# A chunked recurrence without levels, and experts' rows in groups of three tiles turned by VectorE

## The chip, the cores and the metric

The kernel runs on one core of one Trainium2 chip. The time is that of one execution on the device, in microseconds (us). Everything is float32.

## What is computed

Two blocks follow each other. The first is a gated linear recurrence over 4 batches x 8 heads, 768 tokens and a head dimension of 48; the second sends each of the 3,072 tokens (a row of 384 values, all heads side by side) to the one of eight experts with the largest logit.

```
f = 1 / (1 + exp(-f_logit))
for t in range(S):                       # per batch and head, state is 48 x 48
    state = f[t][:, None] * state + outer(k[t], v[t])
    y[t] = q[t] @ state
x = y as (3072, 384)
e = argmax(x @ w_gate)                   # w_gate: 384 x 8
out = softmax(x @ w_gate)[e] * (relu(x @ w1[e]) @ w2[e])   # w1: 384 x 1024, w2: 1024 x 384
```

## The kernel before, in words

**Recurrence (L146 to L373).** A chunk is 128 tokens of one batch, 24 in all, two batches half a chunk apart (`steps`, `advance`, L344 to L373). Tokens lie on partitions when loaded; `turned` (L178) transposes f, q and k on TensorE, two heads to a 128-row tile. Seven levels (L224) then build the scores: at each, four products of 128 columns (L227), the query factors multiplied on VectorE (L234), the key factors on GpSimd (L236), the block totals (L238), and a masked copy into the score tile (L240). Each level needs the factors of the one before. The chunk's outputs are eight products of the scores (L250) and, after the first chunk, eight of the state (L260); the state takes a transpose of the keys (L272), a product (L278) and a sum (L293). The rows are transposed again for the gate's logits (L301, L306).

**Routing (`route`, L309).** Once for each batch of six chunks: expert, place within the expert's region of a scratch tensor `xs` in memory, gate. Rows are scattered to `xs` by an indirect DMA that GpSimd issues (L130).

**Plan (L376 to L416).** After the last chunk a tile of padding is scattered behind each expert's rows, and VectorE works out for each of 31 tiles which expert and which row it has. 31 is the most that any routing can need; all run.

**Experts (L418 to L462).** Tile by tile: SyncE (SP) reads two registers and loads the tile's 128 rows and its expert's first weights (1.5 MB, L430); TensorE transposes the rows (L434); 24 products of 128 columns (L443), ReLU on ScalarE and VectorE, eight of 384 columns with second weights that were loaded during the recurrence (L457), the gate on VectorE (L461), a scatter to the output. The program's order on each engine is the order in which a scheduler took the statements as written.

Of the kernel before, what the change touches and what calls it, by code (L numbers as in the profile page):

```python
# [19 lines left out]
C = 128  # tokens in a chunk, and in a tile of an expert's rows  # L20
NC = S // C
HP = H // 2
DP = 64  # rows that a head takes in the layouts with the head dim on partitions
DM = H * D
KD = DM // 128
N = B * S
E, F = 8, 1024
NF = F // 128
LEVELS = [1 << i for i in range(7)]
STAGES = len(LEVELS) + 3  # of a chunk  # L30

REGION = N + C  # rows of an expert in the scratch: all tokens and a tile of padding
DUMMY = E * REGION  # a tile of padding rows for the tiles that no expert needs
ROWS = DUMMY + C
# [3 lines left out]
FAR = 1 << 20  # the token of a padding row  # L38


def _consts():
# [3 lines left out]
    def row(v):  # L45
# [8 lines left out]
        "eidx": row(e),  # L54
        "tiles": row(np.arange(N // C) * C),
        "i": row(np.arange(NT)),
        "irow": row(np.arange(NT) * C - DUMMY),
        "p": p[:, None],
    }
    # By level: columns are the second halves of the blocks of 2m tokens, rows  # L60
    # that count are the first half of the same block.
    m = {}
    for lv in LEVELS:
        t = p[p // lv % 2 == 1]
        m[lv] = (p[:, None] // (2 * lv) == t[None] // (2 * lv)) & (p[:, None] // lv % 2 == 0)
    m[0] = np.eye(128)
# [17 lines left out]
def kernel(  # L84
    ctx: ExitStack,
    tc: tile.TileContext,
    q: bass.AP,
    k: bass.AP,
    v: bass.AP,
    f_logit: bass.AP,  # L90
# [11 lines left out]
    nc.scalar.dma_start(fpack, nc.inline_tensor(fv, name="c_fpack").ap())  # L102
    nc.scalar.dma_start(mpack, nc.inline_tensor(mv, name="c_mpack").ap())
# [5 lines left out]
    def mask(lv):  # L109
        a, w = mat[lv]  # L110
        return mpack[:, a : a + w]

    ident = const("ident")

    xs = nc.dram_tensor("xs", (ROWS, ROW), F32, kind="Internal").ap()

    w2r = cpool.tile([128, E, NF, DM], F32, name="w2r")
    wg = cpool.tile([128, KD, E], F32, name="wg")
    nc.scalar.dma_start(wg, moe_w_gate.rearrange("(k p) e -> p k e", p=128))
    pad = cpool.tile([128, ROW], F32, name="pad")  # L120
    tok = cpool.tile([128, N // C], I32, name="tok")
    base = cpool.tile([128, B * NC + 1, E], F32, name="base")
# [366 lines left out]
```

## Time and profile before

| | us |
|---|---|
| median of three runs | 1058.12 |
| the three runs | 1054.77, 1085.23, 1058.12 |
| span of the profiled execution, first to last instruction | 1046.0 |
| recurrence and routing in it | 0 to 656 |
| last routing, padding, plan, first loads | 656 to 688 |
| 31 experts' tiles | 688 to 1038 |

The span leaves out what lies around the program's instructions; the profiled execution has no time of its own beside its span, so the runs stand for it. PE is TensorE's products and PEld its weight loads, which overlap them; DVE is VectorE, ACT ScalarE, POOL GpSimd and SP SyncE. A float32 product shows as two records of each kind.

### The profile page before, as it was taken

What the parts mean: (1) busy time and instruction counts of PE and PEld (TensorE: products, weight loads), DVE (VectorE), ACT (ScalarE), POOL (GpSimd) and SP (SyncE); (2) the same over time, 40 slices, a digit from 0 to 9 for tenths busy, and PEclk for the clock granted to TensorE, in tenths of its full rate; (3) what the DMA queues carried; (4) which work ended last, traced back from release to release, by engine and by line L of the source; (5) the groups of instructions that cost most, each with busy time, mean ns of one, the idle gap of its engine ahead of it and who ended that gap; (6) DMA issues with size and microseconds to landing.
All of it is one profiled execution on the core that took longest, in us unless ns stands there. A gap on an engine that the chain in (4) does not pass through costs nothing.

```text
span 1046.0 us, 13595 instructions
## 1 busy us (share of the span) xinstructions
PE 822.6 (79%) x5077; PEld 712.2 (68%) x5077; DVE 519.0 (50%) x1022; ACT 115.9 (11%) x205; POOL 207.4 (20%) x267
## 2 busy tenths in 40 slices
PE   5767777777776677777777777079999999999996
PEld 4667666667676666766776766067787787787775
DVE  7686777775666777667777763311111111111111
ACT  2020111111111211111111110000000000000000
POOL 2221222221214422222222213500010010010010
PEclk8797899996878799888899975579999999999999
DMA  9364112210112211111110001355445445545540
GB/s 224 129 213 150 31 31 42 41 33 17 22 31 78 71 31 39 29 25 31 31 31 8 1 0 48 110 213 205 161 154 188 181 158 191 174 155 175 190 157 1
DMA packets 129952, 99.27 MB, mean 95 GB/s; under 512 B 102734, under 2 KB 115313, under 8 KB 129888
## 3 DMA queue, kind: packets, MB, share of 16 engines
q1 hardware_dynamic: 125024, 86.58, 27.7%
q0 software_dynamic: 4032, 11.28, 3.0%
q8 instruction: 42, 0.69, 0.3%
q10 hardware_dynamic: 832, 0.54, 0.2%
q14 instruction: 22, 0.18, 0.1%
HBM read 86.90 MB, written 12.85 MB: 95 GB/s over the span
## 4 chain that ended last, share of the span: by engine, by line
issue 35%; DVE 30%; PE 28%; POOL 4%; DMA 1%; ACT 1%; SPq 0%; POOLq 0%; ACTq 0%
DVE qg L234 14%; PE lps L227 12%; DVE at L240 7%; PE y L250 5%; PE y L260 4%; DVE qg L221 3%; POOL out_dram L130 3%; DVE at L210 3%; DVE tots L238 2%; PE dp L278 2%; PE lp L306 2%; PE dps L207 1%; PE hps L443 1%; DMA w1t<-in_moe_w_dram 1%; POOL xs L130 1%
## 5 line engine op out<-in xcount | busy, mean ns | idle before, releaser
L227 PE MATMUL lps<-qg,kg 128*128 128x128 f32 x1344 | 240.7, 335 | 125.8 <-DVE qg L221 76.6
L227 PEld LDWEIGHTS lps<-qg,kg 128*128 128x128 f32 x1344 | 214.4, 239 | 147.6 <-issue 80.2
L234 DVE TENSOR_TENSOR qg<-qg,tots 64x256 f32<-64x256 f32 x288 | 161.1, 559 | 53.8 <-PE lps L227 50.0
L443 PEld LDWEIGHTS hps<-xT,w1t 128*128 128x128 f32 x1488 | 172.1, 194 | 20.9 <-DVE xT L436 11.4
L443 PE MATMUL hps<-xT,w1t 128*128 128x128 f32 x1488 | 175.2, 278 | 13.0 <-DVE xT L436 7.8
L236 POOL TENSOR_TENSOR kg<-kg,tots 128x256 f32<-128x256 f32 x140 | 110.1, 786 | 336.6 <-PE lps L227 296.6
L457 PE MATMUL yps<-w2r,hT 128*128 x496 | 165.1, 486 | 0.0
L240 DVE COPY_PREDICATED at<-mpack,lps 128x512 f32<-128x512 uint8 x168 | 148.0, 881 | 4.5
L457 PEld LDWEIGHTS yps<-w2r,hT 128*128 128x128 f32 x496 | 91.9, 190 | 57.5
L453 DVE TENSOR_SCALAR hT<-hps 128x512 f32<-128x512 f32 x31 | 21.4, 692 | 164.8 <-PE hps L443 90.1
L130 POOL DMA_INDIRECT out_dram<-ysb,xrow x31 | 30.1, 972 | 333.1 <-DVE ysb L461 307.5
L461 DVE TENSOR_SCALAR ysb<-yps,xrow 128x384 f32<-128x384 f32 x31 | 19.1, 617 | 136.2 <-PE yps L457 136.2
L250 PE MATMUL y<-vld,at 128*128 128x48 f32 x384 | 51.0, 289 | 24.6 <-DVE at L240 24.3
L250 PEld LDWEIGHTS y<-vld,at 128*128 128x128 f32 x384 | 47.9, 203 | 30.2 <-DVE at L240 30.2
L207 PE MATMUL dps<-qg,kg 128*128 128x256 f32 x192 | 50.8, 410 | 17.9 <-ACT kg L200 17.9
L451 ACT ACTIVATE hT<-hps 128x512 f32<-128x512 f32 x31 | 18.5, 597 | 356.6 <-PE hps L443 356.6
L207 PEld LDWEIGHTS dps<-qg,kg 128*128 128x128 f32 x192 | 36.7, 201 | 27.9 <-ACT kg L200 23.3
L234 DVE TENSOR_TENSOR qg<-qg,ft 64x256 f32<-64x256 f32 x48 | 32.3, 672 | 41.3 <-PE lps L227 40.5
L260 PE MATMUL y<-state,qg 128*128 128x48 f32 x320 | 48.1, 313 | 0.0
L260 PEld LDWEIGHTS y<-state,qg 128*128 128x128 f32 x320 | 46.2, 230 | 0.0
L236 POOL TENSOR_TENSOR kg<-kg,ft 128x256 f32<-128x256 f32 x24 | 23.9, 996 | 98.4 <-PE lps L227 98.4
L274 ACT COPY kn<-kp 128x512 f32<-128x512 f32 x20 | 11.7, 586 | 244.4 <-PE kp L272 244.4
(86 smaller groups left out, 567.0 us busy)
## 6 DMA issues: line engine op xcount, KB each, us to landing
w1t<-in_moe_w_dram SPq DMA_DIRECT2D x31, 1536.0 KB, 6.6
w2r<-in_moe_w_dram SPq DMA_DIRECT2D x8, 1536.0 KB, 8.7
xrow<-xs SPq DMA_DIRECT2D x31, 200.0 KB, 2.4
fld<-in_f_logit_dram SPq DMA_DIRECT2D x24, 192.0 KB, 2.7
qld<-in_q_dram SPq DMA_DIRECT2D x24, 192.0 KB, 3.2
kld<-in_k_dram SPq DMA_DIRECT2D x24, 192.0 KB, 2.8
vld<-in_v_dram SPq DMA_DIRECT2D x24, 192.0 KB, 2.7
out_dram<-ysb,xrow POOLq DMA_INDIRECT x31, 2.6
```

The lines of the kernel that those rows point to most:

```text
L130: ins = nc.gpsimd.indirect_dma_start(out=dst, out_offset=bass.IndirectOffsetOnAxis(ap=idx, axis=0), in_=src, in_offset=None, bounds_check= ...
L207: nc.tensor.matmul(ps[:, j], lhsT=kg[:, hp, :], rhs=qg[:, hp], start=True, stop=True)
L210: nc.vector.copy_predicated(at[:, 4 * g : 4 * g + 4, :], _bc(mask(0), 1, 4), ps.rearrange("p j a t -> p (j a) t"),)
L221: nc.vector.tensor_tensor(qg[r, :, a, :], qg[r, :, a, :], ft[r], op=OP.mult)
L227: nc.tensor.matmul(ps[:, hp], lhsT=kg[:, hp, :], rhs=half(qg[:, hp], m, 1), start=True, stop=True)
L234: nc.vector.tensor_tensor(q1, q1, _bc(two[r, :, :, 0], 3, m), op=OP.mult)
L236: nc.gpsimd.tensor_tensor(k0, k0, _bc(two[:, :, :, 1], 3, m), op=OP.mult)
L240: nc.vector.copy_predicated(half(at, m, 1), _bc(mask(m).rearrange("p (n r) -> p n r", r=m), 1, H), ps.rearrange("p h a (n r) -> p (h a) n ...
L250: nc.tensor.matmul(y[:, h * D : h * D + D], lhsT=at[:, h, :], rhs=vt[:, h * D : h * D + D], start=h == 0, stop=c == 0, skip_group_check=True,)
L260: nc.tensor.matmul(y[:, h * D : h * D + D], lhsT=qg[:, h // 2, h % 2, :], rhs=state[:, h // 2, :], start=False, stop=True, skip_group_chec ...
L443: nc.tensor.matmul(hp[:, f, :], lhsT=w1t[:, j, o : o + 128], rhs=xT[:, j, :], start=j == 0, stop=j == KD - 1,)
L457: nc.tensor.matmul(yp, lhsT=hT[:, f, :], rhs=w2r[:, ds(er, 1), f, :], start=f == 0, stop=f == NF - 1)
```

## The change

It is a new program for both stages; the fallback at its end is the only part that works as a loop on the chip.

- **Inputs** are laid out on the host: q, k and f come with the head dimension on partitions (a pair of heads, 64 rows each, zeros above 48), by units of 128 tokens x two batches x eight heads; v with tokens on partitions. There are 12 units; the transposes of q, k and f go.
- **Recurrence.** The levels go. Per unit: `steps` (ScalarE: exp, then ln, which gives -log f), `total` (VectorE: a running sum over each chunk's tokens), `growth` and `decay` (ScalarE: exp of the sum and of its negative), k times the one on GpSimd, q times the other on VectorE. One product for each head then gives its scores (`score`), copied through one causal mask. `keys` transposes k (TensorE), `keep` copies it (ScalarE), `within` and `before` write the outputs with the head dimension on partitions, `added` and `update` make the next state, `settle` copies the outputs (ScalarE), `rows` turns them back into rows together with their logits by one product with a matrix of ones and gate weights, `lay` copies the rows (ScalarE). Routing is by groups of two units (one at the end). The order on every engine is that of the statements: iteration n works on units n + 3 to n - 2.
- **Early tiles.** The first 128 rows of experts 0 and 1 are complete before the recurrence ends; their two tiles run in the last iterations and after them. Padding is written by SP, whose registers take each expert's end (`load_pads`).
- **Experts.** The expert of a tile is fixed: three tiles each, two for experts 0 and 1, one product of 384 (256) columns for the first weights, which are loaded once per expert, as the second ones are. Rows come from memory in blocks of 32 x 96 (`load_blocks`: four loads, and one for tokens and gates), which one VectorE transpose in squares of 32 turns (`turn`).
- **Spill.** An expert's rows beyond 384 go in squares of 32 rows. Two *quads* of four squares, each with its own expert's weights (3 MB a square), run beside experts 4 and 7: four products write 32 rows of the result each, eight transposes, four products again (`widen_quad`, `turn_quad`, `narrow_quad`; `fetch` loads them half an expert at a time).
- **Fallback.** A branch at the end reads a flag on all engines. The flag is set where a running sum or a routing goes beyond what the fixed program holds; then loops do it again.

The diff, cut to what sets the order and the sizes:

```diff
-LEVELS = [1 << i for i in range(7)]
...
-NT = N // C + E - 1  # the most tiles that any routing needs
...
+T = 32
+QUADS = 2
+SLOTS = 4 * QUADS
+SPILL = 4
...
+WITH = {4: 0, E - 1: 1}
+FETCH = {2: 0, 9: 1}
...
+EARLY = 2
...
+    def load_blocks(to, rows):
+        for j in range(128 // BK):
+            nc.sync.dma_start(
+                to[BK * j : BK * j + BK],
+                rows[:, DB * j : DB * j + DB].rearrange("(i c) m -> c i m", c=BK),
+            )
+    def load_rows(row, n=1):
+        rows = xs[ds(row, n * C)] if not isinstance(row, int) else xs[row : row + n * C]
+        x = rowp.tile([128, TILES * C // BK, DB], F32, name="xrow")[:, 0 : n * C // BK]
+        tg = rowp.tile([128, TILES, USED - TOK], F32, name="tg")[:, 0:n]
+        load_blocks(x, rows)
+        nc.sync.dma_start(tg, rows[:, TOK:USED].rearrange("(t p) r -> p t r", p=C))
+        return {"n": n, "x": x, "tg": tg}
...
+        nc.vector.transpose(
+            x["xT"].rearrange("p k (i c) -> p i k c", c=BK),
+            x["x"].rearrange("p i (r k) -> p i k r", k=KD),
+        )
...
+        per = 4 // n
+        for b in blocks:
+            i, f = divmod(b, per)
+            if f == 0:
+                x["h"] = bank(i)[:, 0 : per * n * C].rearrange("p (f c) -> p f c", f=per)
+            for j in range(KD):
+                nc.tensor.matmul(
+                    x["h"][:, f],
+                    lhsT=w[0][:, j, b * 128 : b * 128 + 128],
+                    rhs=x["xT"][:, j],
+                    start=j == 0,
+                    stop=j == KD - 1,
+                )
...
+    def put(x, t, yp, group):
+        ysb = ep.tile([128, DM], F32, name="ysb")
+        nc.vector.tensor_scalar(ysb, yp, x["tg"][:, t, 1:2], None, op0=OP.mult)
+        scatter(out, x["dst"][:, t : t + 1], ysb, N - 1, group)
...
+            g = x["g"][:, part, 1:CR]
+            most = gsum[:, u, 1 if part == ab[1] else 0]
+            nc.scalar.activation(
+                g, x["f"][:, part], AF.Exp, scale=-1.0, accum_out=most.unsqueeze(1)
+            )
+            nc.scalar.activation(g, g, AF.Ln, bias=1.0)
...
+            nc.vector.tensor_tensor_scan(
+                x["sum"][:, part].rearrange("p s c -> p (s c)"),
+                x["g"][:, part].rearrange("p s c -> p (s c)"),
+                cap[:, part].rearrange("p s c -> p (s c)"),
+                0.0,
+                OP.add,
+                OP.min,
+            )
...
+            nc.scalar.activation(x["r"][:, part], x["sum"][:, part, 1:CR], AF.Exp)
...
+        def by_r(u, part=whole):
+            k = units[u]["k"][:, part]
+            nc.gpsimd.tensor_tensor(k, k, units[u]["r"][:, part], op=OP.mult)
...
+            nc.scalar.activation(
+                x["dec"][:, part], x["sum"][:, part, 1:CR], AF.Exp, scale=-1.0
+            )
...
+            nc.vector.tensor_tensor(q, q, x["dec"][:, part], op=OP.mult)
...
+        def score(u, a):
+            x = units[u]
+            x["at"] = scores[u % 2]
+            ps = [pss.tile([128, HP, C], F32, name="s") for h in range(2)]
+            for p, h, r in heads():
+                s = HP * a + p
+                nc.tensor.matmul(
+                    ps[h][:, p], lhsT=x["k"][r, s], rhs=x["q"][r, s], start=True, stop=True
                 )
+            for h in range(2):
+                nc.vector.copy_predicated(x["at"][:, a, h], _bc(causal, 1, HP), ps[h])
...
+        def within(u, a):
+            x = units[u]
+            if a == 0:
+                x["yt"] = yt
+            for p, h, _ in heads():
                 nc.tensor.matmul(
+                    x["yt"][DP * (h ^ a) : DP * (h ^ a) + D, a, p],
+                    lhsT=x["v"][:, a, 2 * p + h],
+                    rhs=x["at"][:, a, h, p],
+                    start=p == 0,
+                    stop=x["old"] is None,
                     skip_group_check=True,
                 )
+        def before(u):
+            x = units[u]
+            if x["old"] is None:
+                return
+            for p in range(HP):
+                for h in range(2):
+                    for a in range(2):
+                        r = slice(DP * h, DP * h + D)
+                        to = DP * (h ^ a)
+                        nc.tensor.matmul(
+                            x["yt"][to : to + D, a, p],
+                            lhsT=x["old"][r, HP * a + p],
+                            rhs=x["q"][r, HP * a + p],
+                            start=False,
+                            stop=True,
+                            skip_group_check=True,
+                        )
+        def added(u):
+            x = units[u]
+            x["dp"] = turns("dp", [128, SEG, D])
+            for a in range(2):
+                for p, h, r in heads():
+                    s = HP * a + p
                     nc.tensor.matmul(
+                        x["dp"][r, s],
+                        lhsT=x["kn"][:, s, r],
+                        rhs=x["v"][:, a, 2 * p + h],
+                        start=s == 0,
                         stop=True,
                         skip_group_check=True,
                     )
...
+        for n in range(NU + 2):
+            here, back, last = n, n - 1, n - 2
+            rt = None
+            if here < NU:
+                units[here]["old"] = states[here % 2]
+            if 0 <= last:
+                settle(last)
+            if here < NU:
+                score(here, 0)
+            if 0 < n and n + 1 < NU:
+                by_r(n + 1)
+                ends(n + 1)
+            if later:
+                settled(*later)
+                later = None
+            if decayed:
+                decayed()
+                decayed = None
+            if sends:
+                now = sends if n >= NU - 1 else sends[:1]
+                for send in now:
+                    send()
...
+            elif here < NU:
+                if n == 1:
+                    added(0)
+                    decayed = update(0)
+                keys(here)
+                keep(here)
+                score(here, 1)
+            if 0 < n and n + 2 < NU:
+                total(n + 2)
+            if 0 <= last:
+                rt = rows(last)
+                if rt:
+                    rt.choose()
+            if 0 < n and n + 1 < NU:
+                decay(n + 1)
+                last_decay(n + 1)
+            if 0 < n and n + 3 < NU:
+                steps(n + 3)
+            if 0 <= last:
+                lay(last)
+            if rt:
+                rt.weigh()
+            if 0 < n and n + 2 < NU:
+                growth(n + 2)
+            for a in range(2):
+                if 0 <= back < NU:
+                    within(back, a)
+            if n == NU + 1:
+                widen(soon[0], weights[0], early_h, range(3, 7))
+            if n == NU:
+                for x in soon:
+                    turn_early(x)
+            if 0 <= back < NU:
+                before(back)
+            if 0 < n and n + 1 < NU:
+                for part in ab:
+                    by_decay(n + 1, part)
...
+            if 0 < here < NU and here // 2 < NC - 1:
+                added(here)
+                decayed = update(here)
+            if rt:
+                rt.count(turns("rp", [128, 2, rt.n, E], n < NU - 2))
+                later = (n, rt)
+                if n >= NU:
+                    settled(*later)
+                    later = None
+            if n == NU:
+                early_h = early_banks()
+                widen(soon[0], weights[0], early_h, range(3))
+            if n == NU + 1:
+                widen(soon[0], weights[0], early_h, range(7, NF))
+            if 0 < n and n + 3 < NU:
+                load(n + 3, "k")
+            if n + 2 < NU:
...
+            if n in (8, 10):
+                load_first_weights((n - 8) // 2)
+                load_second_weights((n - 8) // 2)
+            if n == NU - 1:
+                soon = [load_rows(first[e]) for e in range(EARLY)]
...
+        over, okc = share(), sums()
+        rows_of = {}
+        for e in range(E):
+            load_pads(e)
+            if e < 2:
+                rows_of[e] = load_expert(e)
+        narrow_early(soon[0], weights[0])
+        widen(soon[1], weights[1], early_banks(), range(NF))
+        check(okc, over)
+        turn(rows_of[0])
+        narrow_early(soon[1], weights[1])
...
+            hp = [bank(b).rearrange("p (f c) -> p f c", c=C) for b in range(2)]
+            hq = qp.tile([128, 2, 4, C], F32, name="hq")
+            for b in range(2):
+                for j in range(KD):
+                    for g, r in pieces():
+                        nc.tensor.matmul(
+                            hp[b][r].rearrange("p f c -> p (f c)"),
+                            lhsT=x["xT"][:, j, r],
+                            rhs=x["w"][0][:, g, j, b * 512 : b * 512 + 512],
+                            start=j == 0,
+                            stop=j == KD - 1,
+                            skip_group_check=True,
+                        )
...
+        for e in range(E):
+            x, w = rows_of[e], weights[e]
+            x["hT"] = qp.tile([128, NF, TILES * C], F32, name="hT")[:, :, 0 : x["n"] * C]
+            widen(x, w, bank, range(NF))
+            if e in WITH:
+                widen_quad(quad)
+            if e + 1 < E:
+                turn(rows_of[e + 1])
+            if e + 1 in WITH:
+                turn(quad, qp)
+            if e + 2 < E:
+                rows_of[e + 2] = load_expert(e + 2)
+                load_first_weights(e + 2)
+            fetch(2 * e)
+            for t in range(x["n"]):
+                if e in WITH and t == 1:
+                    turn_quad(quad)
+                if e in WITH and t == 2:
+                    narrow_quad(quad)
+                narrow_late(x, t, w)
+            if e + 2 < E:
+                load_second_weights(e + 2)
+            fetch(2 * e + 1)
+    todo = nc.values_load(fixi[0:1, 0:1], min_val=0, max_val=1)
+    with tc.If(todo > 0):
```

## Rows read from the trace of the kernel before

**Rows 1.** The page: busy us (share of span) by engine; granted clock, 40 slices.

```profile
PE 822.6 (79%) x5077; PEld 712.2 (68%) x5077; DVE 519.0 (50%) x1022; ACT 115.9 (11%) x205; POOL 207.4 (20%) x267
...
PEclk8797899996878799888899975579999999999999
```

**Rows 2.** Windows: us; PE, PEld, DVE, ACT, POOL busy; clock; DMA share; GB/s.

```profile
150.00:550.00 400.00, 296.35 (x1915) 272.67 (x1913) 283.29 (x561) 62.23 (x111) 103.12 (x131) 0.86 0.17 37
656.00:688.00 32.00, 2.19 (x8) 1.72 (x9) 7.32 (x33) 0.00 (x0) 13.72 (x14) 0.50 0.49 179
...
718.00:1030.00 312.00, 304.73 (x1854) 241.36 (x1853) 49.64 (x84) 16.13 (x27) 27.22 (x28) 1.00 0.48 168
```

**Rows 3.** The page: the chain that ended last, by engine and line.

```profile
issue 35%; DVE 30%; PE 28%; POOL 4%; DMA 1%; ACT 1%; SPq 0%; POOLq 0%; ACTq 0%
DVE qg L234 14%; PE lps L227 12%; DVE at L240 7%; PE y L250 5%; PE y L260 4%; DVE qg L221 3%; POOL out_dram L130 3%; DVE at L210 3%; DVE tots L238 2%; PE dp L278 2%; PE lp L306 2%; PE dps L207 1%; PE hps L443 1%; DMA w1t<-in_moe_w_dram 1%; POOL xs L130 1%
```

**Rows 4.** Waits: who waited for whom, us in total, times, longest.

```profile
PE lps L227 <- DVE qg L221: 76.6, 24, 3.3
```

**Rows 5.** Timeline, experts' tiles: start, us, engine, line, count.

```profile
687.74 7.96 PE L443 MATMUL hps<-xT,w1t 128*128 128x128 f32 x48 [5.18 <-issue]
...
802.59 5.52 PE L443 MATMUL hps<-xT,w1t 128*128 128x128 f32 x48
...
807.95 5.33 PE L457 MATMUL yps<-w2r,hT 128*128 x16
...
813.11 0.82 PE L434 MATMUL etp<-fpack,xrow 128*128 128x128 f32 x6
```

**Rows 6.** Timeline, products of 48 columns at either clock.

```profile
245.73 1.99 PE L250 MATMUL y<-vld,at 128*128 128x48 f32 x16 [1.54 <-DVE at L240]
...
620.87 3.61 PE L260 MATMUL y<-state,qg 128*128 128x48 f32 x16
```

**Rows 7.** Groups by form: busy us, mean ns | idle before, releasers.

```profile
L236 POOL TENSOR_TENSOR kg<-kg,tots 128x256 f32<-128x256 f32 x140 | 110.1, 786 | 336.6 <-PE lps L227 296.6 <-issue 26.3 <-DVE tots L238 6.8
...
L210 DVE COPY_PREDICATED at<-mpack,dps 128x512 f32<-128x512 uint8 x48 | 33.8, 724 | 4.9 <-PE dps L207 4.5
L221 DVE TENSOR_TENSOR qg<-qg,ft 64x512 f32<-64x512 f32 x48 | 32.6, 679 | 0.7
...
L130 POOL DMA_INDIRECT xs<-xr,posi x24 | 23.9, 994 | 13.7 <-DVE tots L238 5.5 <-issue 5.5 <-DVE posi L331 1.7
...
L274 ACT COPY kn<-kp 128x512 f32<-128x512 f32 x20 | 11.7, 586 | 244.4 <-PE kp L272 244.4
...
L268 ACT COPY xr<-y 128x384 f32<-128x384 f32 x24 | 11.5, 479 | 152.4 <-PE y L260 141.6 <-PE y L250 7.8 <-DVE at L240 3.0
...
L238 DVE TENSOR_TENSOR tots<-ft 128x256 f32<-128x256 f32 x24 | 10.0, 415 | 2.0 <-ACT ft L194 2.0
L287 POOL TENSOR_TENSOR state<-state,tots 128x192 f32<-128x192 f32 x16 | 8.6, 538 | 35.5 <-DVE tots L238 35.5
...
L314 DVE TENSOR_REDUCE mx<-lg 128x6 f32<-128x48 f32 x4 | 0.8, 204 | 0.1
```

**Rows 8.** Timeline, the end.

```profile
1037.61 0.49 PE L457 MATMUL yps<-w2r,hT 128*128 x1
...
1039.03 0.97 POOL L130 DMA_INDIRECT out_dram<-ysb,xrow  x1 [9.55 <-DVE ysb L461]
```

**Rows 9.** DMA of the first 30 us in 40 slices.

```profile
GB/s 0 0 50 278 255 282 225 237 290 304 222 220 187 200 256 201 215 220 222 128 229 365 303 360 398 329 292 155 103 237 201 204 232 207 238 250 379 352 381 401
```

**Rows 10.** Timeline, TensorE's first work.

```profile
4.37 1.08 PE L181 MATMUL fp<-fpack,fld 128*128 128x128 f32 x4 [4.37 <-DMA fld<-in_f_logit_dram]
```

**Rows 11.** DMA issues: count, KB each, median us to landing.

```profile
w1t<-in_moe_w_dram SPq DMA_DIRECT2D x31, 1536.0 KB, 6.6
...
xrow<-xs SPq DMA_DIRECT2D x31, 200.0 KB, 2.4
...
xs<-xr,posi POOLq DMA_INDIRECT x24, 2.6
```

More of the change, by code (lines that the diff above doesn't have):

```diff
@@ L53, in _consts @@
         "first": row(e * REGION),
[L54 to L57, printed above, removed]
+        "full": row(e * REGION + C),
+        "most": row(e * REGION + MOST),
+        "spill": row((e[:, None] * REGION + TILES * C + np.arange(SPILL) * T).ravel()),
+        "spillat": row((e[:, None] * REGION + TILES * C + np.arange(SPILL) * T).ravel() - NONE),
+        "spillof": row(np.repeat(e, SPILL)),
+        "slots": row(1 + np.arange(SLOTS)),
+        "tok": p[:, None] + np.arange(N // C)[None] * C,
         "p": p[:, None],
+        "sel": np.stack([p < DP, p >= DP], 1),
     }
[L62 to L66, printed above, removed]
+    sel = np.zeros((128, HP, WX))
+    for a in range(2):
+        sel[DP * a + np.arange(D), :, E + D * a + np.arange(D)] = 1.0
+    f["rows"] = sel.reshape(128, HP * WX)
+    for n in (1, 2, 4):
+        f[f"run{n}"] = row(np.tile(np.arange(n + 1) > 0, E))
+    m = {"causal": np.triu(np.ones((128, 128)))}
     packs = []
@@ L86 @@
     tc: tile.TileContext,
[L87 to L90, printed above, removed]
+    qT: bass.AP,
+    kT: bass.AP,
+    fT: bass.AP,
+    vT: bass.AP,
+    qu: bass.AP,
+    ku: bass.AP,
+    fu: bass.AP,
+    vu: bass.AP,
     moe_w_gate: bass.AP,
@@ new lines, in load @@
+        def load(u, names, parts=(slice(None),)):
+            x = units[u]
+            for n in names:
+                src = {"q": qu, "k": ku, "f": fu, "v": vu}[n]
+                if n == "v":
+                    x[n] = ld.tile([128, 2, H, D], F32, name=n, bufs=3)
+                else:
+                    x[n] = held[n][u % len(held[n])]
+                for part in parts:
+                    nc.sync.dma_start(x[n][:, part], src[u][:, part])
+        whole, ab = slice(0, SEG), (slice(0, HP), slice(HP, SEG))
@@ L373 @@
-        while running:
-            advance()
-    end = base[:, B * NC]
-    idx = cpool.tile([128, E], I32, name="idx")
-    nc.vector.tensor_scalar(idx, end, const("p"), None, op0=OP.add)
-    for e in range(E):
-        scatter(xs, idx[:, e : e + 1], pad, ROWS - 1, "xs")
-    one = slice(0, 1)
-    cnt = cpool.tile([1, E], F32, name="cnt")
-    nc.vector.tensor_tensor(cnt, end[one], const("first")[one], op=OP.subtract)
-    more = cpool.tile([1, E, N // C], F32, name="more")
-    nc.vector.tensor_tensor(
-        more, _bc(cnt, 2, N // C), _bc(const("tiles")[one], 1, E), op=OP.is_gt
-    )
```

930 lines of the change are left out of this document (650 added, 280 removed).

## The prediction

> **What bounds the kernel now.** First the page: TensorE is busy 79% of the span and VectorE 50%, and the slices of its granted clock read 5 to 9 tenths until slice 27 and 9 or more from there on [rows 1]. So the span has two halves with different limits, and the windows say which [rows 2]. In the recurrence (0 to 656 us) TensorE is busy 296 of 400 us at a mean clock of 0.86 and VectorE 283: neither is full. The chain that ended last [rows 3] alternates there between the seven levels' masks and factors on VectorE (L234, L240) and their products (L227). TensorE's 76.6 us of waiting for L221 in 24 chunks is the sign of it [rows 4]: a latency chain. From 656 to 688 us TensorE works 2.2 of 32 us, at a granted clock of 0.50 (1.2 of 2.4 GHz), while row numbers are computed, scattered and planned. From 688 us on it is busy 304.7 of 312 us at full clock: the experts are bound by TensorE itself, 31 tiles in 350 us.
>
> **Prices.** At full clock 48 instructions of 128 columns took 5.52 us (115 ns each), 16 of 384 columns 5.33 us (333 ns), 6 transposes 0.82 us (137 ns); the first tile, met at half clock, took 7.96 us [rows 5]. Sixteen instructions of only 48 columns took 1.99 us at full clock, 124 ns each, and 3.61 us at half [rows 6]: there the load of 128 weight columns sets the pace. A float32 product is two such instructions. For the other engines [rows 7]: a masked copy of 512 elements 0.72 us, VectorE products of 256 and 512 elements 0.42 and 0.68, small routing operations 0.2, ScalarE passes of 384 and 512 elements 0.48 and 0.59 (so 1.0 for 1,024), a GpSimd product of 256 elements 0.79 and of 192 0.54, a scatter 0.99 plus about 0.3 to the next.
>
> **The recurrence.** Levels, device transposes of q, k and f, and the step of half a chunk all go; a unit (128 tokens, two batches, 16 heads) takes one iteration. TensorE per iteration: scores, 32 instructions of 128 columns whose loads are 128 columns wide, 32 x 124 ns = 3.9 us; eight transposes 1.1; `within`, 32 of 128 columns, 48-column weights, outputs in alternate halves of the array; `before`, the same with half the rows too; `added`, 32 of 48 columns with 64-column weights; `rows`, 16 at 124 ns = 2.0; counting 0.25 a unit. No row shows two halves of the array at work together. The ends for `within` are 32 x 115 ns = 3.7 us, one after another, and half of it, 1.85; for `before` 3.7 and a quarter, 0.9; for `added` 3.9 (the 124 ns row) and 32 x 115 x 48/128 = 1.4. I take 1.85, 1.85 and 2.0: two 64-column halves fill the array as one 128-column product does, and that is the row in hand; half a weight load at half 124 ns gives 2.0. Eight changes of shape an iteration: nothing in an expert's tile now; at most the tail of one record beyond the pace, 0.49 - 0.33 = 0.16 us each [rows 8], 1.3 in all; I take 0.5. The sum is 13.5 us, with ends 10 and 19.
>
> The others fit beneath it. ScalarE: four passes of 1,024 (4.0), four copies of 512 (2.3), up to three for `lay` (1.4): 7.8 us. VectorE: four masked copies 2.9, two products 1.4, state 0.55, about ten small operations 2.0, and the running sum over 1,032 elements, which no row shows at length: 1.2 us at the product's pace, 2.4 at half of it; 8.0 to 9.2. GpSimd: the product by r 3.1, state 1.1, two scatters 2.6, small copies 0.6: 7.4. If TensorE's cover went, VectorE would come next at 9.2. Loads are 1.9 MB an iteration, 140 GB/s, where the same queue moved 300 to 400 GB/s [rows 9].
>
> On the scores a page speaks against the packing: the Trainium skill, "TensorE: Matmul & The Clock Gate", section "LDWEIGHTS (loading the stationary operand)", has a load cost by its columns whatever its rows, so two 64-row loads cost two full ones; the 48-column products at 124 ns agree, and by that rule the scores stay at 3.9.
>
> **Start.** TensorE's first product now starts at 4.4 us, when a 0.19 MB load lands [rows 10]. A first half of f is 0.25 MB, so ScalarE starts near 4.5 us and is the bound: eight half passes each for units 0 and 1 (9.6 us), a unit's two copies (1.2), unit 2's and 3's first passes (4.0) and a last 1.0 make 15.8; then GpSimd's 3.1 and VectorE's 1.4: iteration 2 begins at 26 us. **Iterations 2 to 11:** 10 x 13.5, less `added` in the last two (2 x 2.0), 131 us: 157. **Iterations 12 and 13** hold settling (1.2), `rows`, `within`, `before` and three of eight blocks of the first early tile (0.69 each), 9 us; then settling, `rows` and five blocks, 7 us: 173.
>
> **Between the stages.** The 32 us with an idle TensorE become 5.33 + 5.52 + 5.33 = 16.2 us of early tiles: 189. Beneath them lie the last routing (3.7), two scatters (2.6 and 2.6 to land [rows 11]), pads and then rows through SP (2.7 and 2.4) and turning on VectorE (1,152 elements, 1.3): 15.3 from the last `rows`, against 5 x 0.69 + 16.2 = 19.6. Pads move from POOL's queue to SP's, where experts 0's and 1's rows stand behind their value loads. The load of an expert's tokens and gates reuses a buffer that the earlier tile's `put` frees; all of SP's later loads queue behind it, up to a whole second product. First weights behind it are due 32 us later and land in 6.6; the cover is four times the cost. If it went, 6.6 us per expert would be exposed.
>
> **Experts.** 22 tiles remain: 18 in threes, two pairs. First products: 48 x 333 ns = 16.0 us for three tiles, 48 of 256 columns 10.7; second products 5.33 a tile. 6 x 32.0 + 2 x 21.4 = 235 us. Turning on VectorE takes three transposes a tile from TensorE (0.41 us) and lies beside other work. The reference's inputs give 343 to 443 rows an expert, hence six of eight spill squares used; both quads run anyway. A quad has 48 instructions of 512 columns (444 ns), 64 of 384 and eight transposes: one after another 21.3 + 21.3 + 1.1 = 43.7 us; four column groups at once 5.3 + 5.3 + 1.1 = 11.7. I take 15, the packed end with a quarter more and changes of shape, for the same reason as in `within`: 30 for two. Quad weights are 24 MB more; with the experts' they need 13.5 MB in the 48 us before the second quad, 281 GB/s, under the 300 to 400 shown. So TensorE ends at 189 + 235 + 30 = 454.
>
> **End.** From the last product to the end now 8.0 us (1,046.0 - 1,038.1) [rows 8]; the branch on every engine has no row: nothing to 12, I take 4. The new span is 466 us. The profiled span is 1,046.0; the median of the runs shown, 1,058.1, stands 12 above it, and I keep that: **478 us**.
>
> **Rivals.**
> 1. *No packing.* Halves and quarters run one after another: 19 us an iteration and 43.7 a quad, so 10 x 5.5 + 2 x 28.7 + 4 in the tail = 116 more, 594 us. For it: no row shows packing. Against: outputs lie in disjoint halves and the order alternates them. 0.10.
> 2. *Loads in parallel too.* Scores fall to 1.95 us, iterations to 11.5: 458 us; with every lower end, 10 us an iteration and 11.7 a quad, 436. The Trainium skill, "TensorEngine Tiling (Array Packing)", section "Key Properties", lets different tiles load and multiply in parallel, which would be this case; the same section drains the engine at each change of tiling mode, which is the 1.3 us end above; no run here shows either. 0.15.
> 3. *Waits and the clock.* Engine-to-engine waits, as L221's now, leave TensorE gaps and the mean clock stays 0.86: 13.5/0.86 = 15.7 us, 22 more, 500 us; if every iteration ran at half clock, 125 more, over 600. The shorter chain speaks against it, four other engines at 7 to 9 us an iteration for it. 0.22.
> 4. *The fallback runs (slower).* The branch at the end redoes everything in loops if a unit's sum of log decays passes ln(1e18) = 41.4 or routing doesn't fit. Its 768 inner passes each chain a load and a store (about 2.5 us each) and three VectorE passes of 768 elements (0.9 each), 8 us or more: over 6,000 us in all. It decides from the first such sum. On the reference's inputs the largest is 21.1, experts 0 and 1 have their 128 rows long before unit 10, and 443 is under 512. 0.02.
>
> Forecast 0.51. **Range:** 440 to 560: it takes in rivals 2 and 3 but for their far ends and leaves out 1 and 4. Within 2% of before is about what a measurement cannot tell from no change; no case lies there but an overflow of routing alone, which adds a second pass over the experts near the old 350 us and more. Faster 0.97, same 0.01, slower 0.02.
>
> **What would show it.** TensorE busy over 85% between 26 and 157 us at a clock near 1.0, iterations of 13.5 us, `s` products at 124 ns a piece and `yt` at half of 115 or less: else the packing is wrong. Early tiles end near 189 us with no gap before the experts; the experts' stage lasts 265 us, each quad about 15. A gap before a quad with its weights as releaser would be SP's queue. A wait of TensorE for VectorE or ScalarE in each iteration is rival 3. The forecast is wrong if the recurrence ends outside 140 to 190 us or a quad takes over 25.

## The result, and the profile after

The changed kernel took **411.93 us** (median of four runs, 411.07 to 412.84) against 1,062.67 us beside it: 0.388 of the time before (95% interval 0.385 to 0.391). The forecast was 478 us with a range from 440, so the direction was right and the time lies 28 us below the range. The profiled execution's span is 409.2 us, 2.7 below the median.

The page after (busy time, granted clock, DMA rate by slice, and the chain that ended last by engine and line):

```profile
PE 395.6 (97%) x2906; PEld 276.6 (68%) x2906; DVE 161.1 (39%) x342; ACT 106.0 (26%) x196; POOL 113.0 (28%) x120
...
PEclk9989999999999999999999999999999999999998
...
GB/s 281 360 213 378 323 265 240 239 192 358 400 159 113 152 187 325 88 340 63 166 220 344 388 393 270 375 301 20 33 301 38 96 296 388 404 398 135 20 29 15
...
PE 92%; ACT 2%; DVE 2%; POOL 1%; issue 0%; POOLq 0%; ACTq 0%; DVEq 0%
PE yps L320 28%; PE hps L304 28%; PE xp L620 6%; PE s L511 5%; PE yt L537 5%; PE s L304 3%; PE yps L1009 3%; PE hps L981 3%; PE yp L320 3%; PE yt L558 3%; PE kp L524 2%; PE dp L574 2%; PE warmth L667 2%; DVE sum L462 1%; ACT r L476 1%; POOL rend L483 1%
```

Where [rows 1, 3] had a chain shared by VectorE and TensorE, TensorE alone now carries 92% of it. The windows say the same of each stage (us; PE, PEld, DVE, ACT, POOL busy; clock; DMA share; GB/s): the recurrence, the tail with the early tiles, the experts.

```profile
30.00:120.00 90.00, 89.18 (x1424) 80.23 (x1422) 73.70 (x165) 61.05 (x113) 59.99 (x62) 1.00 0.82 291
120.00:150.00 30.00, 29.29 (x236) 24.20 (x236) 16.06 (x74) 4.85 (x13) 9.49 (x14) 1.00 0.44 131
150.00:400.70 250.70, 250.68 (x976) 147.55 (x974) 45.86 (x73) 16.55 (x32) 23.17 (x24) 1.00 0.68 225
```

Against [rows 2]: the recurrence runs TensorE 99% of the time at full clock, no longer 74% at 0.86, the wait of [rows 4] has no successor, and the 32 us with 2.2 us of work are gone. One iteration on TensorE (start, us, engine, line, count), to the start of the next:

```profile
64.46 1.16 PE L511 MATMUL s<-q,k 64*128 64x128 f32 x16
65.56 1.09 PE L524 MATMUL kp<-fpack,k 128*128 128x128 f32 x8
66.58 1.16 PE L511 MATMUL s<-q,k 64*128 64x128 f32 x16
67.67 2.03 PE L620 MATMUL xp<-fpack,ys 128*128 128x104 f32 x16
69.63 1.96 PE L537 MATMUL yt<-at,v 128*48 128x128 f32 x32
71.52 1.09 PE L558 MATMUL yt<-q,state 48*48 48x128 f32 x32
72.54 1.14 PE L574 MATMUL dp<-v,kn 128*64 128x48 f32 x32
73.60 1.16 PE L511 MATMUL s<-q,k 64*128 64x128 f32 x16
```

That is 9.14 us; every second iteration also counts for the routing (L220, L221) and takes 9.71. So 9.4 on average, where 13.5 were forecast. The scores of 16 instructions take 1.09 us from start to start, not 16 x 124 ns = 1.98. The starts of single instructions, from the same trace, show how (ns from each start to the next; the last number of a part runs to the next part's first start):

```
scores  L511  6 207 7 105 6 105 7 105 7 105 6 105 7 105 7 202
keys    L524  164 109 110 109 109 109 109 203
within  L537  7 140 6 103 7 102 7 102 7 102 7 103 ... 6 103 7 102 7 202
before  L558  7 7 6 127 7 6 7 89 7 6 7 89 ... 7 6 7 199
added   L574  7 86 7 52 6 52 7 51 7 52 ... 7 52 6 52 7 151
quad    L1009 7 7 6 327 7 6 7 303 6 7 7 302 7 6 7 303 ... 7 6 7 416
```

Products of different halves start 7 ns apart, and four quarters too: such a **round** lasts as long as one of its instructions alone (the experiments below show them alone): 109 to 112 ns at 128 columns, 58 for `added` (48 columns, loads of 64 of the 128 weight columns), 322 at 384. And at each change of shape the last step is about 0.1 us longer and the first one 0.02 to 0.10.

The later stages, as [rows 5, 8] (the first early tile's second product, then experts 0, 2 and 4 with a quad, and the end):

```profile
132.80 5.33 PE L320 MATMUL yp<-w2t,hT 128*128 128x384 f32 x16
...
149.58 10.63 PE L304 MATMUL hps<-xT,w1t 128*128 128x256 f32 x48 [0.71 <-DVE ysb L331]
...
191.04 15.64 PE L304 MATMUL hps<-xT,w1t 128*128 128x384 f32 x48
206.52 15.64 PE L320 MATMUL yps<-w2t,hT 128*128 128x384 f32 x48
...
268.54 5.36 PE L981 MATMUL hps<-qw,qxT 128*32 128x512 f32 x48
...
279.09 1.04 PE L1000 MATMUL hps<-fpack,hq 128*128 128x128 f32 x8
...
285.22 5.37 PE L1009 MATMUL yps<-qw,hqT 128*32 128x384 f32 x64
290.51 5.43 PE L320 MATMUL yps<-w2t,hT 128*128 128x384 f32 x16
```

```profile
400.72 0.62 DVE L331 TENSOR_SCALAR ysb<-yps,tg 128x384 f32<-128x384 f32 x1 [4.71 <-PE yps L320]
401.61 0.97 POOL L183 DMA_INDIRECT out_dram<-ysb,dst  x1 [4.35 <-DVE ysb L331]
```

The 64 instructions of a quad's second product take as long as 16 of a plain one: four column groups work at once. The only wait of TensorE in the experts' stage is the 0.71 us at its start.

### The profile page after: what moved, and what is told of

Same layout as the page of the kernel before. It is cut to its first block, busy times and chain, and to the rows that moved or that the text cites. A ratio compares the mean times of both kernels' runs of the same rounds, so it can differ in the third digit from the quotient of the medians.

```text
span 409.2 us, 7342 instructions
## 1 busy us (share of the span) xinstructions
PE 395.6 (97%) x2906; PEld 276.6 (68%) x2906; DVE 161.1 (39%) x342; ACT 106.0 (26%) x196; POOL 113.0 (28%) x120
## 4 chain that ended last, share of the span: by engine, by line
PE 92%; ACT 2%; DVE 2%; POOL 1%; issue 0%; POOLq 0%; ACTq 0%; DVEq 0%
PE yps L320 28%; PE hps L304 28%; PE xp L620 6%; PE s L511 5%; PE yt L537 5%; PE s L304 3%; PE yps L1009 3%; PE hps L981 3%; PE yp L320 3%; PE yt L558 3%; PE kp L524 2%; PE dp L574 2%; PE warmth L667 2%; DVE sum L462 1%; ACT r L476 1%; POOL rend L483 1%
## 5 line engine op out<-in xcount | busy, mean ns | idle before, releaser
L320 PE MATMUL yps<-w2t,hT 128*128 128x384 f32 x352 | 115.9, 487 | 0.0
L304 PE MATMUL hps<-xT,w1t 128*128 128x384 f32 (+1 forms) x384 | 115.0, 460 | 0.7 <-DVE ysb L331 0.7
L304 PEld LDWEIGHTS hps<-xT,w1t 128*128 128x128 f32 x384 | 72.9, 190 | 42.1 <-DVE ysb L331 1.3
L320 PEld LDWEIGHTS yps<-w2t,hT 128*128 128x128 f32 x352 | 66.4, 190 | 47.5 <-issue 2.9
L183 POOL DMA_INDIRECT out_dram<-ysb,dst x26 | 25.3, 974 | 240.4 <-DVE ysb L331 240.4
L316 DVE TENSOR_SCALAR hT<-hps 128x384 f32<-128x384 f32 (+1 forms) x28 | 16.2, 577 | 98.2 <-PE hps L304 98.2
L183 POOL DMA_INDIRECT xs<-xr,posi x24 | 32.4, 1349 | 26.6 <-DVE counts L227 12.0
L515 DVE COPY_PREDICATED at<-mpack,s 128x512 f32<-128x512 uint8 x48 | 32.4, 728 | 12.2 <-PE s L511 12.2
L480 POOL TENSOR_TENSOR k<-k,r 128x1024 f32<-128x1024 f32 (+1 forms) x14 | 30.1, 2156 | 22.1 <-ACT r L476 22.0
L511 PE MATMUL s<-q,k 64*128 64x128 f32 x384 | 28.8, 285 | 2.3 <-DVE at L515 1.4
L462 DVE TENSOR_TENSOR_SCAN sum<-g,cap 128x1032 f32<-128x1032 f32 (+1 forms) x14 | 28.4, 2032 | 3.2 <-ACT g L455 3.2
```

Source lines behind the costliest of these rows:

```text
L183: ins = nc.gpsimd.indirect_dma_start(out=dst, out_offset=bass.IndirectOffsetOnAxis(ap=idx, axis=0), in_=src, in_offset=None, bounds_check= ...
L304: nc.tensor.matmul(x["h"][:, f], lhsT=w[0][:, j, b * 128 : b * 128 + 128], rhs=x["xT"][:, j], start=j == 0, stop=j == KD - 1,)
L316: nc.vector.tensor_scalar(to, x["h"], 0.0, None, op0=OP.max)
L320: nc.tensor.matmul(yp, lhsT=x["hT"][:, f, t * C : t * C + C], rhs=w[1][:, f, :], start=f == 0, stop=f == NF - 1,)
L462: nc.vector.tensor_tensor_scan(x["sum"][:, part].rearrange("p s c -> p (s c)"), x["g"][:, part].rearrange("p s c -> p (s c)"), cap[:, part ...
L480: nc.gpsimd.tensor_tensor(k, k, units[u]["r"][:, part], op=OP.mult)
```

## Experiments

Kernels of one set share a chip. The unaltered changed kernel, run again in two other sets, took 416.95 us (415.09 to 418.14, `e7_again`, expected at 411 to 414) and 411.47 us (411.00 to 412.25, `e10_again`): TensorE's experts' stage took 251.1 us in both, and began 5.9 us later in the first, so that the difference lay before it. The set of `e1`, `e2`, `e3` and `e6` holds no unaltered copy. So effects are read from the stage or product that an edit touches, not from totals alone.

**Order of the packed products.** `e1_one_half` issues the same products with four of one half in a row.

```diff
-            return [(p, h, slice(DP * h, DP * h + DP)) for p in range(HP) for h in range(2)]
+            return [(p, h, slice(DP * h, DP * h + DP)) for h in range(2) for p in range(HP)]
...
-            for p in range(HP):
-                for h in range(2):
-                    for a in range(2):
+            for h in range(2):
+                for a in range(2):
+                    for p in range(HP):
```

> Order of issue alone: in the scores, in `within` and `added` four products in the same half of TensorE's array follow each other instead of one in each half by turns, in `before` four in the same quarter. Same products, same operands, same loads. Theory A (two neighbours in different halves run at once, their weight loads too, and only then is an instruction cheap): with 8 instructions in one half before the next, 94 to 115 ns an instruction of 128 columns; scores 3.0 to 3.7 us an iteration instead of 2.2, `within` 3.0 to 3.7 instead of 1.9, `before` 3.0 to 3.4 instead of 1.0, `added` about 1.7 instead of 1.15; iterations 13.5 to 15 us instead of 9.2, in all 455 to 475 us. Theory B (a load of 64 rows or a product of few rows or columns is cheap by itself, whatever stands beside it): scores, `within`, `before` and `added` keep their times and the kernel its 412 us.

449.55 us (448.69 to 450.41). One iteration's packed products:

```profile
64.35 1.71 PE L511 MATMUL s<-q,k 64*128 64x128 f32 x16
...
70.61 2.91 PE L537 MATMUL yt<-at,v 128*48 128x128 f32 x32
73.45 2.51 PE L558 MATMUL yt<-q,state 48*48 48x128 f32 x32
75.89 1.49 PE L574 MATMUL dp<-v,kn 128*64 128x48 f32 x32
```

Same work, same operands, and scores take 1.71 for 1.16, `before` 2.51 for 1.09: the speed comes from neighbours in different parts of the array, not from small products being cheap. Theory A holds and B falls, though the total is below A's range, because some overlap stays at the border of two runs. The steps between starts also give an instruction alone: 112 ns in the scores, 109 in `within` and `before`, 58 to 59 in `added`, as the rounds above.

**The quads, group by group.** In `e2_quad_order` each group finishes its products before the next.

```diff
-                for j in range(KD):
-                    for g, r in pieces():
+                for g, r in pieces():
+                    for j in range(KD):
...
-            for f in range(NF):
-                for g, r in pieces():
+            for g, r in pieces():
+                for f in range(NF):
```

> Order of issue alone: in the two quads all products of one group of 32 columns follow each other, then the next group's, instead of the four groups by turns. Theory A (groups of columns run at once only as neighbours): first products 48 x 427 ns = 20.5 us a quad instead of 5.3, second 64 x 322 ns = 20.6 instead of 5.3, less an overlap at each of the few changes of group; 57 to 61 us more, 469 to 473 us. Theory B (a product with 32 weight columns is four times as fast by itself): nothing changes, 412 us.

447.24 us (446.67 to 447.81):

```profile
274.71 8.98 PE L981 MATMUL hps<-qw,qxT 128*32 128x512 f32 x48
...
295.02 17.05 PE L1009 MATMUL yps<-qw,hqT 128*32 128x384 f32 x64
```

Packing again, but neither product is one after another (A's 20.5): the starts in the second one, where a group has 16 instructions, read

```
347 322 323 322 323 322 323 322 323 322 323 322 6 317 30 292 30 293 30 322 323 ...
```

The trace doesn't say which group a start belongs to; it is read from the steps, a lone 322 ns being one group by itself. After the 13th instruction of a group, the next group's first starts 6 ns behind it, while the 14th to 16th are still to come. **Three instructions of a group can be held back while a later one goes ahead; a fourth blocks the queue.** In `e1_one_half`, with runs of eight, it is the fifth start that has the next half's first 6 ns behind it. Two kernels bear on that.

**Runs of two products** (four instructions) of a half in a row, in scores, `within` and `added`:

```diff
-            return [(p, h, slice(DP * h, DP * h + DP)) for p in range(HP) for h in range(2)]
+            return [(p + o, h, slice(DP * h, DP * h + DP)) for p in range(0, HP, 2) for h in range(2) for o in range(2)]
```

> Order of issue alone: in the scores, `within` and `added` two products in one half, then two in the other. Theory A1 (instructions start strictly in order, so that of a run of 2n instructions in one half only the last runs beside the first of the next): 2n - 1 steps of 107 ns for 2n instructions, so 80 ns an instruction instead of 59 to 68; scores 2.6 us instead of 2.2, `within` 2.6 instead of 1.9, `added` about 0.2 more; iterations 10.4 to 10.6 us, in all 422 to 427 us. Theory A2 (TensorE looks further ahead and takes any product whose half is free): unchanged, 412 us. Theory B: unchanged, and e1_one_half unchanged as well.

420.85 us (418.39 to 421.77). With three held back, a run of four should cost nothing, and it costs little: 1.26, 2.04 and 1.17 us for 1.16, 1.96 and 1.14. A1, strict order, falls by the iterations: 9.45 and 10.03 us for 9.14 and 9.71, 0.3 more where A1 has 1.2. The total alone, near A1's 422 and with no copy beside it, would not decide.

```profile
76.00 1.26 PE L511 MATMUL s<-q,k 64*128 64x128 f32 x16
...
81.37 2.04 PE L537 MATMUL yt<-at,v 128*48 128x128 f32 x32
```

**The second products of the quads in runs** of four instructions (first quad) and eight (second):

```diff
-            for f in range(NF):
-                for g, r in pieces():
+            for f0 in range(0, NF, run):
+                for f, g, r in [(f0 + i, g, r) for g, r in pieces() for i in range(run)]:
...
-                    narrow_quad(quad)
+                    narrow_quad(quad, 2 if WITH[e] == 0 else 4)
```

> Order of issue alone in the second products of the quads: runs of two products (4 instructions) in a group of columns in the first quad, of four products (8) in the second. One product by turns gave 5.3 us a quad, eight in a run 17.0. Theory F (TensorE holds about three instructions ready for a busy group and starts later ones in other groups beside them; worked out from e2_quad_order: 3 x (15 - Q) + 16 steps of 322 ns = 17.0 us gives Q = 2.8): runs of 4 still packed, 5.3 to 5.6 us; runs of 8: (7 x (7 - 2.8) + 8) x 0.322 = 12.0 us. Theory A1 (strictly in order, nothing held): (15 x 3 + 4) x 0.322 = 15.8 and (7 x 7 + 8) x 0.322 = 18.4 us. In all 7 us more than e7_again by F, 24 by A1.

422.97 us (422.85 to 423.08); the two products are

```profile
290.28 5.44 PE L1009 MATMUL yps<-qw,hqT 128*32 128x384 f32 x64
...
395.09 12.01 PE L1009 MATMUL yps<-qw,hqT 128*32 128x384 f32 x64
```

as Theory F had it (5.3 to 5.6, and 12.0); the total is 6.0 us above `e7_again` (7 by F, 24 by A1). The first quad also shows that the three are held for each group and not in all: its first four starts, one in each group, lie within 40 ns (13, 14, 13), and with runs of four, nine earlier instructions must then be waiting.

**Scores in quarters**: each score product cut into two of 64 keys, the second with the 64 queries that its keys can reach (the masked rest is left out). Beside what the cut diff shows, the score tiles take three fixed banks, zeroed once.

```diff
-                nc.tensor.matmul(
-                    ps[h][:, p], lhsT=x["k"][r, s], rhs=x["q"][r, s], start=True, stop=True
-                )
+                for kb in (0, 64):
+                    nc.tensor.matmul(
+                        ps[h][kb : kb + 64, p, kb:C],
+                        lhsT=x["k"][r, s, kb : kb + 64],
+                        rhs=x["q"][r, s, kb:C],
...
```

> Scores by quarters of the array: each head's product is cut into keys 0 to 63 (128 query columns) and keys 64 to 127 (the 64 query columns that the causal mask keeps), so that four products with 64 weight columns each stand in four quarters, and a quarter of the work is left out as masked anyway. Theory G (scores are bound by weight loads of 128 columns, two at a time): 64 instructions an iteration, 32 x (107 + 53)/4 ns = 1.3 us instead of 2.2; VectorE stands at 80% in these iterations, so part of it may come back as waits: 4 to 10 us less than e7_again. Rival H (VectorE's order of masked copies, sums and state sets the iteration once TensorE is faster): no difference, within 2 us. Rival I (more instructions cost more than they pack): slower, scores above 2.2 us.

417.21 us (415.47 to 419.15), as `e7_again` of the same set. Theory G's 1.3 us an iteration is not there; 32 instructions take nearly what 16 took, 1.03 us to the next line for 1.09:

```profile
66.66 1.10 PE L515 MATMUL s<-q,k 64*64 64x128 f32 x32
...
68.71 1.10 PE L515 MATMUL s<-q,k 64*64 64x128 f32 x32
```

The starts (ns; of two that lie 13 or 14 apart the first), told apart by the columns they stream:

```
128 columns  0 160 269 378 487 596 706 815
 64 columns  6 113 171 230 288 381 493 601
```

The two quarters with the early keys still stream 128 columns eight times each, 109 ns apart after a first step of 160; the halves had eight steps of 112 already. The short products don't wait for the long ones: after the first they run ahead and are through with the last two of the long ones still to start. So it is the part of the array with the most columns that sets the time. Quarters with equal shares were not tried.

**First products tile by tile**, 128 columns instead of 384 or 256:

```diff
-            for j in range(KD):
...
-                    rhs=x["xT"][:, j],
+            for t in range(n):
+                for j in range(KD):
...
+                        rhs=x["xT"][:, j, t * C : t * C + C],
```

> Takes back one part of the change: the first products of an expert go tile by tile, 128 columns at a time, where the change has one product of 384 (256). 22 tiles x 48 instructions. In the changed kernel the pace is 107.4 ns per 128 columns at 384 and 111.7 to 115 at 128 (early tiles). Theory C (the weight load just hides behind 128 columns, so the part is worth only the difference in pace): 22 x 48 x 4.3 to 7.6 ns = 4.5 to 8 us more, 416 to 420 us. Rival D (fewer weight loads are what makes the experts' stage fast): at the 124 ns of load-bound products, 17.5 us more, 429 us. Rival E: nothing, 412 us.

419.97 us (419.11 to 420.69); the experts' stage takes 255.4 us for 251.1, 4.3 more, just under Theory C's 4.5 to 8; D's 17.5 and E's nothing fall.

```profile
195.54 16.24 PE L305 MATMUL hps<-xT,w1t 128*128 128x128 f32 x144
211.61 15.65 PE L321 MATMUL yps<-w2t,hT 128*128 128x384 f32 x48
```

144 instructions step at 112 ns (16.07 us to the next line), 48 at 322 (15.48): 0.6 us an expert. Sharing the first product is worth little.

**Rows turned by TensorE** for experts 2 to 7, nine transposes each, with whole rows loaded in one transfer:

```diff
+                nc.tensor.transpose(
+                    tp[:, k], x["whole"][:, t].rearrange("p (r k) -> p k r", k=KD)[:, k], ident
+                )
+            nc.vector.tensor_copy(x["xT"][:, :, t * C : t * C + C], tp)
...
+            elif e + 1 < E:
+                turn_whole(rows_of[e + 1], bank)
...
+                rows_of[e + 2] = load_whole(first[e + 2], TILES)
```

> Takes back one part of the change: the rows of experts 2 to 7 come as whole rows and are turned by TensorE, three transposes a tile, copied from PSUM by VectorE, as the kernel before did. 18 tiles x 3 transposes x 128 to 137 ns = 6.9 to 7.4 us on TensorE, which is never idle there. Theory C (the part is worth just these transposes): 7 to 8 us more than e7_again. Rival D (the first transpose waits for the rows or for a bank, and TensorE stops): 1 us or more an expert on top, 13 us and more. Rival E (four block loads of 384-byte pieces cost what they save): no difference.

422.38 us (421.22 to 424.30), 5.4 above `e7_again` of the same set; the experts' stage takes 257.3 us, 6.2 more.

```profile
214.61 1.18 PE L296 MATMUL hps<-fpack,xrow 128*128 128x128 f32 x9
215.63 15.65 PE L342 MATMUL yps<-w2t,hT 128*128 128x384 f32 x48
```

Each group of nine puts 1.02 us into a TensorE that has no gaps, six times 6.1 us: what turning on VectorE saves. C is nearly met, D and E fall.

**The warm-up left out** (38 products, 76 instructions, on padding at the start, which the prediction did not speak of):

```diff
-            for _ in range(count):
+            for _ in range(0):
```

> The products of the padding square with itself at the start (76 instructions, 12 us of TensorE in the changed kernel's trace before iteration 2) are left out; the output doesn't depend on them. Theory S (ScalarE and the loads set the start, TensorE has cover): the first iterations' products run at the lower level of the clock until TensorE has been busy for a while, each about double, but lie beside ScalarE's passes, which are busy 13 of the 18 us from 10 to 28; iteration 2 begins at 28 to 30 us and the total is 0 to 2 us above an unaltered copy. Theory W (the clock carries the start): without them the 13.6 us of real products before iteration 2 take up to 27, with only 4 us of gaps and 4 us of left-out products to take it up, so iteration 2 begins 5 us or more later, and if the clock stays low in the iterations too, each of them takes up to 18 us and the total grows by tens of us.

> The changed kernel unaltered, for scale on this chip. Where a difference of a few us is only the run, it stands at 410 to 418 us, iterations of 9.2 to 9.5 us, experts' stage 251 us.

413.43 us (412.42 to 414.03) against 411.47 for the copy. First without, then with the warm-up:

```profile
9.33 2.08 PE L511 MATMUL s<-q,k 64*128 64x128 f32 x16 [9.33 <-DVE q L500]
11.34 1.97 PE L524 MATMUL kp<-fpack,k 128*128 128x128 f32 x8
...
29.23 1.16 PE L511 MATMUL s<-q,k 64*128 64x128 f32 x16 [1.64 <-issue]
```

```profile
9.51 1.16 PE L511 MATMUL s<-q,k 64*128 64x128 f32 x16
...
27.66 1.16 PE L511 MATMUL s<-q,k 64*128 64x128 f32 x16 [1.83 <-POOL last L495]
```

The first products run at half pace: the transposes step at 213 ns where the copy has 109, though the profile has no fall of the clock on record there. After a wait of TensorE of 2.2 us, to 16.9 us, the granted clock falls: it reads 0.74 from 15 to 20 and 0.58 from 20 to 25 us (a mix of the levels of 1.2 and 2.4 GHz), where the copy has 1.00. A fall is not tied to the missing warm-up alone: the first profile of the changed kernel, with warm-up and a wait of 1.4 us before 22.2 us, reads 0.83 from 20 to 25. Iteration 2 begins 1.6 us later, as Theory S has it (28 to 30 us) and not W (5 us later or more): most of the loss lies in the shadow of ScalarE and GpSimd.

No altered kernel beats the changed one. What TensorE still spends beside its rounds is the changes of shape; fewer of them were not tried.

## Why the prediction was wrong in size

| step | predicted, us | measured | off by |
|---|---|---|---|
| iteration 2 begins | 26 | 28.0 | +2.0 |
| iterations 2 to 11 | 131 | 91.8 | -39.2 |
| iterations 12 and 13 | 16 | 13.0 | -3.0 |
| early tiles, to the experts | 16.2 | 16.8 | +0.6 |
| experts and quads | 265 | 251.1 | -13.9 |
| end | 12 | 8.5 | -3.5 |
| around the span | 12 | 2.7 | -9.3 |
| sum | 478 | 412 | -66 |

The recurrence ended at 132.8 us, outside the 140 to 190 that the prediction named as its test; a quad took 11.5.

**The failed step is the price of the packed products in the recurrence.** In rounds, from the starts above, an iteration holds: scores 2 x 8 x 112 ns = 1.79 us (3.9 predicted), keys 0.87 (1.1), `within` 16 x 109 = 1.75 (1.85), `before` 8 x 109 = 0.87 (1.85), `added` 16 x 58 = 0.93 (2.0), `rows` 16 x 112 = 1.79 (2.0). That is 8.0 us; the 9.14 from start to start leave 1.14 for seven changes of shape, 0.16 each, the upper end of that term and not the 0.5 taken. That end was the tail of a record; whether the two are one thing no run shows. So -4.7 and +0.6 an iteration.

Two things went wrong there. `before` and `added` were put between their ends by an argument on area ("two 64-column halves fill the array as one 128-column product does"). But a product of `before` fills a quarter, and four run at once; `e1_one_half`, by order alone, loses that. `added` came out below even its lower end of 1.4, which was its 32 instructions one after another at the price of their columns: alone one takes 58 ns, but two run at once. And the scores were held at 124 ns an instruction because their weight loads were taken one after another. Loads of two row halves run side by side: 16 of them in eight rounds of 112 ns. The 124 itself was a record with its tail, divided: the starts of those same 16 instructions in the kernel before step at 112. The Trainium skill, "TensorE: Matmul & The Clock Gate", section "LDWEIGHTS (loading the stationary operand)", has the cost by columns whatever the rows; within one half the trace agrees (one load of 128 columns a step of 112 ns), across two halves the sum of such costs, as the prediction had it, is wrong here. The Trainium skill, "TensorEngine Tiling (Array Packing)", section "Key Properties", agrees on both counts: tiles load and multiply in parallel, and a change of mode costs time, 202 ns for 105 and 416 for 322 at the last step. That the engine drains there no run shows by itself.

**Rival 2** was therefore the mechanism, with a chance of 0.15; its far end, 436 us, took every lower end. The lower edge of the range, 440, was above it, and the result lies 24 us below it still, by the iterations (9.4 us for 10) and by terms that this sum left as they were. The 12 us around the span were the spread of the runs before (1,054.8 to 1,085.2), not a cost: in each run of the changed kernel the time is 1.8 to 1.9 us above the span. The end grew by 0.6 us (8.5 for 7.9), which leaves little for the branch. The rows' record lengths (16 x 333 ns) carry the last instruction's tail, so the steps between starts, 322 ns at 384 columns and 216 at 256, give 7.5 of the 13.9 us in the experts. The rest is the quads: 11.5 us, 11.9 with the longer steps beside them, for 15. What held the start up by 2.0 us was not taken apart, and the smallest expert has 335 rows, not 343, which moves nothing here.

**Rival 1** (no packing) and **rival 3** (waits, clock) fell: rounds are visible, and TensorE waits 0.8 us in 90, for ScalarE, at a clock of 1.00. The fallback did not run.

**What held.** The recurrence did become bound by TensorE, with VectorE next: 73.7 us of 90, its running sum at 2.36 us, the upper of the two prices. The gap between the stages closed. SP's loads, which waited 62.9 us in all for buffers that `put` frees, left TensorE no gap, as the cover of an expert was argued to allow. VectorE's turning lies beside other work:

```profile
L462 DVE TENSOR_TENSOR_SCAN sum<-g,cap 128x1032 f32<-128x1032 f32 x10 | 23.6, 2357 | 0.9 <-ACT g L455 0.9
...
L288 DVE STREAM_TRANSPOSE xT<-xrow 128x1152 f32<-128x1152 f32 x6 | 10.5, 1745 | 0.0
```

Which part of the 650 us comes from which part of the change was not taken apart by undoing the recurrence; the stages give it: recurrence 656 to 133 us, the gap 32 to 17 with two tiles in it, experts 350 to 251.

## What to carry to other kernels

Price packed products by rounds: as many instructions as there are free parts of the array run at once, each at the pace that it has alone, and the part with the most columns sets the time; then add 0.16 us for each change of shape. Take paces from steps between starts, not from the length of a record, and where several unknowns hang on one mechanism, let the range hold all their low ends at once. Alternate the parts; runs of two float32 products of one part cost little (0.3 us an iteration), longer ones much.

## What the runs showed of the hardware that was not expected

- TensorE holds back three instructions for each busy part of the array while later ones for another part start: the 13th start in `e2_quad_order` is followed after 6 ns by the next group's. The Trainium skill, "TensorE: Matmul & The Clock Gate", section "The mechanism", speaks of a window 64 deep in which weight loads are pulled ahead; no run here shows that depth, and between groups the starts of products themselves leave the program's order.
- Between products of one full shape there is no extra step at all: 48 and 48 instructions of 384 columns follow each other at 322 ns across L304 and L320. It is a change of shape that costs.
- Products of one part don't wait for a longer one beside them in another part: in `e9_quarter_scores` the last short one starts at 601 ns and the last long one at 815.
- Without warm-up the scores of the start take 2.08 us for 1.16, and the whole kernel 2.0 us more.
